# Step 0 of a gated scan loads f, k and q with four tokens a partition and works by halves of heads

## The chip, the cores and the metric

The kernel runs on one core of a Trainium2 chip. The metric is the device time in microseconds (us). A core has five engines that run side by side: TensorE (PE in the profile) multiplies matrices, VectorE (DVE), ScalarE (ACT) and GpSimd (POOL) work element by element, and SyncE (SP) issues transfers to the DMA queues. TensorE writes to eight PSUM banks of 128 x 512 floats. Everything else lies in SBUF, which has 128 partitions.

## The reference

A gated linear recurrence gives 384 features per token, and a gated two-layer network (ReGLU) follows. There are 4 batches, 8 heads, 768 tokens and head width 48; the network is 384 to 1536 to 384.

```python
f = 1.0 / (1.0 + np.exp(-f_logit))
state = np.zeros((B, H, D, D), dtype=np.float32)
for t in range(S):
    state = f[:, :, t, :, None] * state + np.einsum('bhd,bhe->bhde', k[:, :, t], v[:, :, t])
    y[:, :, t] = np.einsum('bhd,bhde->bhe', q[:, :, t], state)
# x: y with its heads side by side, (B*S, 384)
out = (np.maximum(x @ w_gate, 0.0) * (x @ w_val)) @ w_out
```

## The kernel before

The tokens are cut into six chunks of 128, here called steps 0 to 5, each for four batches. Within a chunk the recurrence is done as attention: the running sum L of -log f over the tokens comes from a product with a triangle of ones, q is scaled by exp(-L) and k by exp(L) (the "hats"), and the scores of q against k are masked by the triangle. y is the masked scores times v, plus q times the old state. The state is carried from step to step.

Nothing waits on an order found at run time. The program lists all operations with assumed durations, a small list scheduler (`Plan`) puts them in an order for each engine and gives them PSUM banks, and each engine then runs its list in that order, with semaphores where one needs another. So the assumed durations set the order, not the time.

For one batch of one step (`attention(c, b)`):

```python
sc.activation(fl, fl, AF.Exp, scale=-1.0)            # f: exp, then ln(1 + .)   [L416, L419]
sc.activation(bo, fl, AF.Ln, bias=1.0)
te.matmul(bc.ap[:, 0:HD], tri[:, :], bn[:, :, 0:D])  # running sums            [L426]
...                                                  # totals with "ones"      [L428]
sc.activation(ex[:, 1, :], bc.ap[:, 0:HD], AF.Exp, scale=1.0)    # for k       [L435]
sc.activation(ex[:, 0, :], bc.ap[:, 0:HD], AF.Exp, scale=-1.0)   # for q       [L437]
...                                                  # decay of the state      [L441]
hk = k * ex[:, 1];  hq = q * ex[:, 0]                # VectorE in step 0, else GpSimd [L447, L451]
gp.tensor_copy(vout, vin)                            # v, cast and padded      [L456]
if c < n_pe_transposed:      # 3                     # steps 0 to 2
    te.transpose(...)  # 8 of 128x128, k then q      [L466]
    ve.tensor_copy(qkT, tp)                          # out of PSUM             [L471]
else:                                                # steps 3 to 5
    sy.dma_start(qkT, hats, transpose=True)          # a DMA transposes        [L475]
te.matmul(s, kT, qT)   # 8, scores                   [L486]
ve.tensor_tensor(ptm, s, tri, ALU.mult)              # 2, mask                 [L492]
te.matmul(y, ...)      # from the old state and from v  [L514; L521 and L525 in steps 3 to 5]
sc.activation(xT, y, AF.Copy)                        # steps 0 to 2            [L532]
...                                                  # steps 3 to 5: copy [L539], then a DMA transposes [L541]
te.matmul(kv, hats_k, v)   # 4, new state            [L551]
...                                                  # step 0: VectorE [L561]; else VectorE, GpSimd [L565, L567]
```

The projections of a step take blocks j of 128 hidden features, 12 in all, with all four batches side by side (512 columns), in step 1 with two at a time (256):

```python
te.matmul(gate, wg_block, xT)  # 3    [L583]
sc.activation(relu, gate, AF.Relu)  # [L589]
te.matmul(val, wv_block, xT)   # 3    [L583]
ve.tensor_tensor(gT, relu, val, ALU.mult)  # [L593]
...
te.matmul(o, gT, wo)           # 12 a batch, output rows  [L604]
sc.activation(osb, o, AF.Copy)           # [L612]; stored by a DMA [L615]
```

The loads of step 0 are one DMA a batch and tensor (192 KB in rows of 48 floats), those of the later steps one for two batches (384 KB). The weights, nine parts of 384 KB in bf16, are issued by GpSimd (L370).

Of the kernel before, what the change touches and what calls it, by code (L numbers as in the profile page):

```python
# [11 lines left out]
class Op:  # L12
# [4 lines left out]
                 "after", "follows", "flow", "goal")  # L17

    def __init__(self, eng, emit, reads, writes, occ, lat, prio, opens=(), after=(), follows=()):
        self.eng, self.emit, self.reads, self.writes = eng, emit, reads, writes  # L20
        self.occ, self.lat, self.prio, self.opens = occ, lat, prio, list(opens)
        self.after, self.follows = list(after), list(follows)
        self.users = []
        self.inc = False
        self.sem = None
        self.val = 0
        self.start = None
        self.flow = None

# [11 lines left out]
class Plan:  # L41
# [4 lines left out]
    def __init__(self, limits):  # L46
        self.ops = []
        self.limits = limits

# [38 lines left out]
    def schedule(self, banks):  # L88
        self.link()
        for op in self.ops:  # L90
            op.n_left = len(op.deps)
            op.ready = 0.0
            for d in op.deps:
                d.users.append(op)
        free = {e: 0.0 for e in self.ENGINES}
# [5 lines left out]
        slots = [{"ap": ap, "tile": None, "at": 0.0} for ap in banks]  # L101
# [113 lines left out]
def bass_hgrn2_outer__then__ffn_reglu_kernel(  # L215
# [10 lines left out]
    n_pe_transposed = 3  # L226
    load_batches = 2
    flight = 3
    n_tiled = 3
    wsteps = 3  # L230
    early = ("f0.0.1 f0.1.2 f0.2.3 f0.3.4 k0.0.1 q0.0.1 v0.0.1 k0.1.2 q0.1.2 v0.1.2 k0.2.3 q0.2.3 "
             "v0.2.3 k0.3.4 q0.3.4 v0.3.4 wg0 wv0 wg1 wv1 wg2 wv2 f1.0.2 k1.0.2 q1.0.2 v1.0.2 wo0 wo1 "
             "wo2 f1.2.4 k1.2.4 q1.2.4 v1.2.4").split()
    lag = 3.0
    first_hats = ['DVE', 'DVE']
    groups = [(0,0,4,1),(1,0,2,0),(1,2,4,0),(2,0,4,0),(3,0,4,0),(4,0,4,0),(5,0,4,0)]
# [15 lines left out]
    NL = 3  # L252
    ld = {n: [sb(f"{n}_in{i}", [128, B, H, D], F32) for i in range(NL)] for n in "fkqv"}
    NB = 3
    bneg = [sb(f"bneg{i}", [128, 2, H, 64], BF16) for i in range(NB)]
    NE = 3
    expo = [sb(f"expo{i}", [128, 2, HD], F32) for i in range(NE)]
    NH = 6
    hats = [sb(f"hats{i}", [128, 2, H, 64], BF16) for i in range(NH)]
    NQ = 6  # L260
    qkT = [sb(f"qkT{i}", [128, 2, NP, C], BF16) for i in range(NQ)]
    NM = 3
    ptm = [sb(f"ptm{i}", [128, 2, NP, C], BF16) for i in range(NM)]
# [3 lines left out]
    NA = 8  # L267
    dec = [sb(f"dec{i}", [128, NP, 2], F32) for i in range(NA)]
    NN = 4
    xn = [sb(f"xn{i}", [128, HD], BF16) for i in range(NN)]  # L270
    NS = 4
# [12 lines left out]
    tri = sb("tri", [128, C], BF16)  # L284
    ident = sb("ident", [128, 128], BF16)
    ones = sb("ones", [128, 1], BF16)
    banks = [nc.alloc_psum_tensor(f"ps{i}", [128, 512], F32) for i in range(8)]

    pl = Plan({"bc": 1, "tp": 1, "s": 2, "y": 1, "kv": 1, "f": 4})
    add = pl.add  # L290
    gp, ve, sc, te, sy = nc.gpsimd, nc.vector, nc.scalar, nc.tensor, nc.sync

    def pe_t(*cols):
        return sum(max(n, 64) / 2400.0 + 0.0025 for n in cols)
# [3 lines left out]
    def act_t(n):  # L298
        return dict(occ=0.1 + n / 1200.0, lat=0.2)

    def dve_t(n):
        return dict(occ=0.08 + n / 960.0, lat=0.2)

    def pool_t(n):
        return dict(occ=0.15 + n * 2.2 / 1200.0, lat=0.2)


    add("POOL", lambda: gp.memset(tri[:], 1.0), [], ["tri"], occ=0.2, prio=-9)
    add("POOL", lambda: gp.affine_select(out=tri[:], in_=tri[:], compare_op=ALU.is_ge, fill=0.0, base=0,
                                         pattern=[[1, 128]], channel_multiplier=-1),  # L310
        ["tri"], ["tri"], occ=0.3, prio=-9)
    add("POOL", lambda: gp.memset(ident[:], 0.0), [], ["ident"], occ=0.2, prio=-8)
    add("POOL", lambda: gp.affine_select(out=ident[:], in_=ident[:], compare_op=ALU.not_equal, fill=1.0,
                                         base=0, pattern=[[-1, 128]], channel_multiplier=1),
        ["ident"], ["ident"], occ=0.3, prio=-8)
    add("POOL", lambda: gp.memset(ones[:], 1.0), [], ["ones"], occ=0.1, prio=-8)

    def zero(eng, e, t, name, cols, prio):
        add(eng, lambda: e.memzero(t), [], [name], occ=0.15 + cols / 2000.0, prio=prio)

    for i in range(NB):
        zero("DVE", ve, bneg[i][:], f"bneg{i}", 1024, -9)
    for i in range(NH):
        zero("DVE", ve, hats[i][:], f"hats{i}", 1024, -8)
    for i in range(NV):
        zero("POOL", gp, vpad[i][:], f"vpad{i}", VW, -7)
    for i in range(NA):
        zero("DVE", ve, dec[i][:], f"dec{i}", 2 * NP, -5)

# [4 lines left out]
    def dma(op, slot, flow):  # L334
# [3 lines left out]
        slots[slot][1] += 16  # L338
# [4 lines left out]

    def load(n, c, b0, b1, after=()):
        last = tails.get("load")
        t = ld[n][c % NL]
        src = bass.AP(tensor=srcs[n].tensor, offset=b0 * H * S * D + c * C * D,
                      ap=[[D, C], [S * D, (b1 - b0) * H], [1, D]])
        dst = t[:, b0:b1, :, :].rearrange("p b h d -> p (b h) d")
        op = add("SP", lambda: sy.dma_start(dst, src), [], [f"{n}{c % NL}_{b}" for b in range(b0, b1)],  # L350
# [3 lines left out]
        dma(op, f"{n}{c % NL}_{b0}{b1}", 1.03 * (b1 - b0))  # L354
# [5 lines left out]
    def load_w(nm, s, after):  # L360
# [4 lines left out]
        else:  # L365
# [4 lines left out]
        op = add("POOL", lambda: gp.dma_start(dst, src), [], [f"{nm}{s}"], occ=0.8, lat=1.0, prio=0, after=after,  # L370
                 follows=[last] if last else [])
        tails["load_w"] = op
        dma(op, f"{nm}{s}", 7.4 / wsteps)
        return op


    done = []
    for item in early:
        weight = item[0] == "w"
        cost, need = 0.0, []  # L380
        for other, flow, op in reversed(done):
            if cost >= lag and other != weight:
                need = [op]
                break
            cost += flow
        if weight:
            op = load_w(item[:2], int(item[2:]), need)
        else:
            c, b0, b1 = (int(x) for x in item[1:].split("."))
            op = load(item[0], c, b0, b1, need)  # L390
        done.append((weight, op.flow, op))
# [6 lines left out]


    def attention(c, b):  # L400
        w = c * B + b
        P = w * 10
        li = c % NL
        bi, bj = (w // 2) % NB, w % 2
        ei, hi, qi, mi, vi, ai = w % NE, w % NH, w % NQ, w % NM, w % NV, w % NA
        xi = c % NX
        fin, kin, qin, vin = (ld[n][li] for n in "fkqv")

        if c == 0:
            parts = [(b, b + 1)]  # L410
        else:
            parts = [(b, b + 2)] if b % 2 == 0 else []
        for b0, b1 in parts:
            fl = fin[:, b0:b1, :, :].rearrange("p b h d -> p (b h) d")
            keys = [f"f{li}_{x}" for x in range(b0, b1)]
            add("ACT", lambda: sc.activation(fl, fl, AF.Exp, scale=-1.0), keys, keys, prio=P,  # L416
                **act_t((b1 - b0) * HD))
            bo = bneg[bi][:, b0 % 2:b0 % 2 + b1 - b0, :, 0:D].rearrange("p b h d -> p (b h) d")
            add("ACT", lambda: sc.activation(bo, fl, AF.Ln, bias=1.0), keys + [f"bneg{bi}"],  # L419
                [f"bn{bi}_{x % 2}" for x in range(b0, b1)], prio=P, **act_t((b1 - b0) * HD))  # L420

        bn = bneg[bi][:, bj, :, :]
        bc = Bank("bc")

        def cum():
            te.matmul(bc.ap[:, 0:HD], tri[:, :], bn[:, :, 0:D])  # L426
            for p in range(NP):
                mm = te.matmul(bc.ap[:, HD + p:HD + p + 1],  # L428
                               bn[:, 2 * p:2 * p + 2, :].rearrange("p h d -> p (h d)"), ones[:, :])
            return mm  # L430
        chain("cum", "PE", cum, ["tri", "ones", f"bneg{bi}", f"bn{bi}_{bj}"], [bc], occ=0.48, lat=PE_L,
            prio=P, opens=[bc])

        ex = expo[ei]
# [3 lines left out]
            [f"expq{ei}"], prio=P + 1, **act_t(HD))  # L438
        if c < NC - 1:
            for j in range(2):  # L440
                add("ACT", lambda lo=64 * j, j=j: sc.activation(dec[ai][lo:lo + 64, :, j], bc.ap[lo:lo + 64, HD:HD + NP],  # L441
                                                                AF.Exp, scale=-1.0),
                    [bc, f"dec{ai}"], [f"dec{ai}_{j}"], prio=P + 2, **act_t(NP))

        hq, hk = hats[hi][:, 0, :, 0:D], hats[hi][:, 1, :, 0:D]
        e0 = first_hats[0] if c == 0 else "POOL"
        add(e0, lambda: (gp if e0 == "POOL" else ve).tensor_tensor(hk, kin[:, b, :, :], ex[:, 1, :].rearrange("p (h d) -> p h d", h=H),  # L447
                                             ALU.mult),
            [f"k{li}_{b}", f"expk{ei}", f"hats{hi}"], [f"hk{hi}"], prio=P + 2, **(pool_t(HD) if e0 == "POOL" else dve_t(HD)))
        e1 = first_hats[1] if c == 0 else "POOL"  # L450
        add(e1, lambda: (gp if e1 == "POOL" else ve).tensor_tensor(hq, qin[:, b, :, :], ex[:, 0, :].rearrange("p (h d) -> p h d", h=H),  # L451
                                             ALU.mult),
            [f"q{li}_{b}", f"expq{ei}", f"hats{hi}"], [f"hq{hi}"], prio=P + 2, **(pool_t(HD) if e1 == "POOL" else dve_t(HD)))
        vp = vpad[vi]
        vout = bass.AP(tensor=vp, offset=0, ap=[[VW, 128], [VSTEP, NP], [64, 2], [1, D]])
# [268 lines left out]
```

## Time and profile before

The median of three runs is 215.39 us (215.35 to 215.4); the profiled execution spans 212.0 us.

| engine | busy, us | share of the span | instructions |
|---|---|---|---|
| PE (matmul) | 186.4 | 88% | 1712 |
| PEld (weight loads, beside PE) | 107.2 | 51% | 1712 |
| DVE | 106.0 | 50% | 189 |
| ACT | 109.5 | 52% | 249 |
| POOL | 72.8 | 34% | 102 |

| queue | packets | MB | share of 16 engines |
|---|---|---|---|
| loads, stores, DMA transposes | 120320 | 27.93 | 64.4% |
| weights | 3984 | 3.54 | 11.2% |

A share of busy time is an average over stages. In the slice rows each digit is a fortieth of the span in tenths of busy time. In the chain each line is a start, a length and what ran or was waited for; "x8" is the number of instructions merged. Line numbers are those in brackets above.

### The profile page before, as it was taken

What the parts mean: (1) busy time and instruction counts of PE and PEld (TensorE: products, weight loads), DVE (VectorE), ACT (ScalarE), POOL (GpSimd) and SP (SyncE); (2) the same over time, 40 slices, a digit from 0 to 9 for tenths busy, and PEclk for the clock granted to TensorE, in tenths of its full rate; (3) what the DMA queues carried; (4) which work ended last, traced back from release to release, by engine and by line L of the source; (5) the groups of instructions that cost most, each with busy time, mean ns of one, the idle gap of its engine ahead of it and who ended that gap; (6) DMA issues with size and microseconds to landing.
All of it is one profiled execution on the core that took longest, in us unless ns stands there. A gap on an engine that the chain in (4) does not pass through costs nothing.

```text
span 212.0 us, 4302 instructions
## 1 busy us (share of the span) xinstructions
PE 186.4 (88%) x1712; PEld 107.2 (51%) x1712; DVE 106.0 (50%) x189; ACT 109.5 (52%) x249; POOL 72.8 (34%) x102
## 2 busy tenths in 40 slices
PE   0365699989999999997993899979999999999994
PEld 0254334455777766853551455535555544445562
DVE  7379525574196867464744357255633333333210
ACT  5940134836676958846753457555243344443411
POOL 3028102192658588853751636326000000000000
PEclk9999999999999999999999699999999999999999
DMA  6999999997999998999998998979422111111112
GB/s 120 217 206 165 196 207 227 152 201 157 200 245 184 188 226 181 172 229 178 212 187 166 216 174 187 184 162 209 111 56 59 37 37 37 40 37 37 37 44 104
DMA packets 124323, 31.73 MB, mean 150 GB/s; under 512 B 117392, under 2 KB 124304, under 8 KB 124304
## 3 DMA queue, kind: packets, MB, share of 16 engines
q1 hardware_dynamic: 120320, 27.93, 64.4%
q0 software_dynamic: 3984, 3.54, 11.2%
q8 instruction: 13, 0.21, 0.4%
q14 instruction: 6, 0.05, 0.1%
HBM read 25.95 MB, written 4.72 MB: 145 GB/s over the span
## 4 chain that ended last, share of the span: by engine, by line
PE 58%; DMA 13%; POOL 8%; ACT 8%; DVE 6%; issue 3%; SPq 2%; POOLq 0%
PE ps L583 30%; PE ps L604 18%; DMA qkT<-hats 7%; DMA f_in<-in_f_logit_dram 7%; POOL hats L451 3%; DVE ptm L492 3%; PE ps L466 3%; POOL hats L447 2%; PE ps L486 2%; ACT relu L589 2%; ACT expo L435 2%; PE ps L514 2%; DVE qkT L471 2%; ACT f_in L416 1%; SPq L350 1%
## 5 line engine op out<-in xcount | busy, mean ns | idle before, releaser
L593 DVE TENSOR_TENSOR gT<-relu,ps 128x512 bf16<-128x512 bf16 (+1 forms) x84 | 50.8, 610 | 63.0 <-PE ps L583 52.9
L589 ACT ACTIVATE relu<-ps 128x512 bf16<-128x512 f32 (+1 forms) x84 | 44.8, 536 | 35.8 <-PE ps L583 35.6
L583 PE MATMUL ps<-xT,wg 128*128 128x512 bf16 (+1 forms) x252 | 61.8, 355 | 0.6 <-ACT xT L532 0.6
L583 PE MATMUL ps<-xT,wv 128*128 128x512 bf16 (+1 forms) x252 | 61.8, 354 | 0.0
L604 PE MATMUL ps<-wo,gT 128*128 128x384 bf16 x288 | 51.4, 326 | 0.0
L492 DVE TENSOR_TENSOR ptm<-ps,tri 128x512 bf16<-128x512 f32 x48 | 30.8, 684 | 14.1 <-PE ps L486 13.9
L604 PEld LDWEIGHTS ps<-wo,gT 128*128 128x128 bf16 x288 | 27.3, 98 | 18.1
L583 PEld LDWEIGHTS ps<-xT,wg 128*128 128x128 bf16 x252 | 23.5, 99 | 21.2 <-issue 1.7
L583 PEld LDWEIGHTS ps<-xT,wv 128*128 128x128 bf16 x252 | 23.3, 98 | 19.2 <-issue 1.3
L612 ACT ACTIVATE osb<-ps 128x384 f32<-128x384 f32 x24 | 11.8, 490 | 31.6 <-PE ps L604 31.5
L447 POOL TENSOR_TENSOR hats<-k_in,expo 128x384 bf16<-128x384 f32 x20 | 20.0, 999 | 20.1 <-ACT expo L435 20.1
L451 POOL TENSOR_TENSOR hats<-q_in,expo 128x384 bf16<-128x384 f32 x20 | 19.9, 998 | 8.6 <-DMA q_in<-in_q_dram 8.6
L567 POOL TENSOR_TENSOR st<-ssum,dec 128x384 bf16<-128x384 f32 x16 | 13.2, 830 | 18.9 <-DVE ssum L565 18.7
L486 PE MATMUL ps<-qkT 48*128 48x128 bf16 x192 | 10.4, 233 | 8.0 <-DMA qkT<-hats 6.7
L435 ACT ACTIVATE expo<-ps 128x384 f32<-128x384 f32 x24 | 11.8, 491 | 8.8 <-PE ps L428 8.7
L426 PE MATMUL ps<-bneg,tri 128*128 128x384 bf16 x24 | 8.6, 359 | 8.4 <-ACT bneg L419 8.4
L456 POOL CAST vpad<-v_in 128x384 bf16<-128x384 f32 x24 | 12.3, 531 | 10.5 <-DMA v_in<-in_v_dram 10.5
L532 ACT ACTIVATE xT<-ps 128x384 bf16<-128x384 f32 x12 | 5.9, 492 | 16.6 <-PE ps L514 16.2
L471 DVE COPY qkT<-ps 128x1024 bf16<-128x1024 bf16 x12 | 8.3, 689 | 12.0 <-PE ps L466 11.9
L486 PEld LDWEIGHTS ps<-qkT 48*128 48x128 bf16 x192 | 5.9, 100 | 14.3 <-DMA qkT<-hats 8.6
L416 ACT ACTIVATE f_in<-f_in 128x768 f32<-128x768 f32 (+1 forms) x14 | 10.4, 747 | 4.5 <-DMA f_in<-in_f_logit_dram 4.2
L437 ACT ACTIVATE expo<-ps 128x384 f32<-128x384 f32 x24 | 11.8, 494 | 0.0
(39 smaller groups left out, 126.3 us busy)
## 6 DMA issues: line engine op xcount, KB each, us to landing
out_dram<-osb SPq DMA_DIRECT2D x24, 192.0 KB, 2.1
f_in<-in_f_logit_dram SPq DMA_DIRECT2D x10, 384.0 KB, 5.5
k_in<-in_k_dram SPq DMA_DIRECT2D x10, 384.0 KB, 5.3
q_in<-in_q_dram SPq DMA_DIRECT2D x10, 384.0 KB, 4.7
v_in<-in_v_dram SPq DMA_DIRECT2D x10, 384.0 KB, 5.1
wg<-in_moe_w_gate_dram POOLq DMA_DIRECT2D x3, 384.0 KB, 7.2
wv<-in_moe_w_val_dram POOLq DMA_DIRECT2D x3, 384.0 KB, 8.3
wo<-in_moe_w_out_dram POOLq DMA_DIRECT2D x3, 384.0 KB, 6.2
```

What stands on the lines that cost most here:

```text
L416: add("ACT", lambda: sc.activation(fl, fl, AF.Exp, scale=-1.0), keys, keys, prio=P, **act_t((b1 - b0) * HD))
L435: add("ACT", lambda: sc.activation(ex[:, 1, :], bc.ap[:, 0:HD], AF.Exp, scale=1.0), [bc], [f"expk{ei}"], prio=P + 1, **act_t(HD))
L447: add(e0, lambda: (gp if e0 == "POOL" else ve).tensor_tensor(hk, kin[:, b, :, :], ex[:, 1, :].rearrange("p (h d) -> p h d", h=H), ALU.mult ...
L451: add(e1, lambda: (gp if e1 == "POOL" else ve).tensor_tensor(hq, qin[:, b, :, :], ex[:, 0, :].rearrange("p (h d) -> p h d", h=H), ALU.mult ...
L471: add("DVE", lambda: ve.tensor_copy(qkT[qi][:, :, :, :].rearrange("p x n t -> p (x n t)"), tp.ap[:, :].bitcast(BF16)), [tp], [f"qkT{qi}"], ...
L486: mm = te.matmul(s.ap[:, p * C:(p + 1) * C], qkT[qi][lo:lo + D, 1, p, :], qkT[qi][lo:lo + D, 0, p, :])
L492: add("DVE", lambda j=j, s=s: ve.tensor_tensor(ptm[mi][:, j, :, :], s.ap[:, :].rearrange("p (n t) -> p n t", n=NP), mask, ALU.mult), [s, " ...
L567: add("POOL", lambda: gp.tensor_tensor(t4(s_new), t4(tmp), rate, ALU.mult), [key] + dk, [f"S{b}_{c % 2}"], prio=P + 8, **pool_t(HD))
L583: mm = te.matmul(bank.ap[:, 0:n], wt[:, kt, j * 128:(j + 1) * 128], xT[xi][:, kt, n0:n1], start=(kt == 0), stop=(kt == NK - 1))
L589: add("ACT", lambda: sc.activation(relu[ri][:, 0:n], gate.ap[:, 0:n], AF.Relu), [gate], [f"relu{ri}"], prio=P, **act_t(n))
L593: add("DVE", lambda: ve.tensor_tensor(gT[gi][:, j, n0:n1], relu[ri][:, 0:n], val.ap[:, 0:n], ALU.mult), [val, f"relu{ri}"], [f"gT{gi}_{j}_ ...
L604: mm = te.matmul(o.ap[:, 0:DM], gT[gi][:, j, b * C:(b + 1) * C], wo[:, j, :], start=(j == 0), stop=(j == NJ - 1))
```

## The change

Its aim is to have the first inputs of the projections sooner and TensorE's clock up when they come, and to plan with other durations.

1. In step 0 f, k and q come with four consecutive tokens of one head in one row of 768 bytes; partition 4r + b holds tokens 4r to 4r + 3 of batch b. All four batches are then worked together, in two halves of four heads. v stays as it was.
2. The running sums of step 0 need two masks for that (`upto`, `below`): ones only where row and column belong to the same batch. k's part of the hats is turned back to natural order later (`attention_back`), when y is done, for the state.
3. TensorE multiplies zeros in the gaps of its plan up to 17 us.
4. The projections of step 0 do blocks 0 to 3 for two batches at a time, the others for four; step 1 blocks 0 to 5 for two, the others for four. The output rows of step 0 are made for two batches together, weight part by weight part.
5. Weights and inputs of step 1 are issued in another order, at other planned times; buffers are counted anew (f two steps, k, q, v two and a half, before three), banks are allotted anew, and the assumed durations are changed.

```diff
-    early = ("f0.0.1 f0.1.2 f0.2.3 f0.3.4 k0.0.1 q0.0.1 v0.0.1 ... wg0 wv0 wg1 wv1 wg2 wv2 f1.0.2 ...").split()
+    first = ("f0 k0 q0 v0.0 v0.1 wg0~8.0 wv0~8.5 wg1~14.5 wv1~15.3 wg2~17.5 wv2~18.3 f1.0@wv1 k1.0 q1.0 v1.0 "
+             "wo0~23 wo1~25.5 f1.1@wo0 k1.1 wo2~28 q1.1 v1.1").split()
...
-    NL = 3
+    NL = {"f": 4, "k": 5, "q": 5, "v": 5}
...
-    pl = Plan({"bc": 1, "tp": 1, "s": 2, "y": 1, "kv": 1, "f": 4})
+    pl = Plan({"bc": 2, "bc4": 4, "tp": 2, "tp4": 4, "s": 4, "y": 2, "kv": 1, "f": 4})
...
-        return dict(occ=0.1 + n / 1200.0, lat=0.2)
+        return dict(occ=0.17 + n / 1150.0, lat=0.2)
...
+    def load_four(n, c):
+            for b in range(B):
+                src = bass.AP(tensor=srcs[n].tensor, offset=b * H * S * D + c * C * D,
+                              ap=[[4 * D, 32], [S * D, H], [1, 4 * D]])
+                dst = bass.AP(tensor=t, offset=b * row + slot_of(n, c, 0) * 2 * HD, ap=[[4 * row, 32], [4 * D, H], [1, 4 * D]])
+                ops.append(sy.dma_start(dst, src))
...
+    def attention_four(c):
+        for hh in range(2):                # halves of heads
+            ... Exp, Ln of 128 x 768
+        for hh in range(2):
+            for z in range(2):             # pairs of the four tokens
+                ... 5 products: upto or below, by bn[:, o]
+            for z in range(2):
+                ... Exp for q to SBUF, Exp for k in its bank
+                e = "DVE" if z else "POOL"
+                ... hats of q by e, hats of k by DVE
+            for x in (1, 0):
+                ... 8 transposes; copy of k's by DVE, of q's by ACT
+            for b in range(0, B, 2):
+                ... 8 scores of two batches, two masks by DVE
+        for j in range(2):
+            masks[(0, 2, j)].follows.append(masks[(1, 0, 1)])
...
+    def attention_back(c, b, behind):
+        ... 4 transposes of k, one copy by DVE, planned behind the batches' y
...
-            dma(op, f"qkT{qi}", 0.9)
+            dma(op, f"qkT{qi}", 1.5)
...
-            dma(op, f"xT{xi}_{b}", 0.35)
+            dma(op, f"xT{xi}_{b}", 0.55)
...
-    groups = [(0,0,4,1),(1,0,2,0),(1,2,4,0),(2,0,4,0),(3,0,4,0),(4,0,4,0),(5,0,4,0)]
+    groups = {0: [(0, 2, range(0, WJ)), (2, 4, range(0, WJ)), (0, 4, range(WJ, NJ))],
+              1: [(0, 2, range(0, 6)), (2, 4, range(0, 6)), (0, 4, range(6, NJ))]}
...
+    warm_until = 17.0
+    def warm():
+        return te.matmul(spare[:, 0:WARM], zeros[:, 0:128], zeros[:, 0:WARM], start=True, stop=True, skip_group_check=True)
+    for op in order["PE"]:
+        gap, each = op.start - at, 0.44 if at < 4.5 else 0.23
+        if begun and op.start <= warm_until:
+            for _ in range(int((gap - 0.05) / each)):
+                busy.append((op, warm))
```

(The lines with "..." behind the plus sign stand for code that is described and cut. Step 5 leaves out the totals that only a next step needs.)

## The prediction

> **What bounds the kernel now.** I read the busy digits by slice first, then the chain of waits in order of time, then the sums by stretch, then the DMA queues. The slices of the page:
>
> ```profile
> PE   0365699989999999997993899979999999999994
> DVE  7379525574196867464744357255633333333210
> PEclk9999999999999999999999699999999999999999
> DMA  6999999997999998999998998979422111111112
> ```
>
> One slice is 5.3 us. TensorE is hardly used in the first five slices and full in nearly all others, so the time is (when the projections start) + (TensorE's work from there) + (its holes) + a tail. The DMA row is full to about 150 us: data arrives only just fast enough, and a shift of TensorE to earlier times must be checked against it. When the projections start is in the chain:
>
> ```profile
> 1.32 3.60 DMA f_in<-in_f_logit_dram
> ...
> 14.53 0.98 PE ps L466 x8
> 15.53 0.69 DVE qkT L471
> ...
> 24.25 1.30 DVE ptm L492 x2
> 25.59 0.65 PE ps L514 x15
> 26.27 0.50 ACT xT L532
> 26.82 13.74 PE ps L583 x57
> ...
> 155.90 1.95 PE ps L604 x12
> 157.85 3.88 PE ps L583 x18
> ```
>
> The first projection is at 26.82, when the fourth batch of step 0 has gone through its transposes, copy, scores, mask and y one after the other. The unhindered rates are in the last two lines: 3.88/18 = 0.2156 us for a 512-column product and 1.95/12 = 0.1625 for a 384-column one. By stretches, TensorE alone (stretch, length, busy and instructions, granted clock, DMA share, GB/s):
>
> ```profile
> 26.80:40.00 13.20, 13.19 (x56) 1.00 1.18 204
> 40.00:60.00 20.00, 19.23 (x226) 1.00 0.93 187
> 60.00:80.00 20.00, 19.74 (x342) 1.00 1.07 209
> 80.00:100.00 20.00, 18.50 (x208) 1.00 1.05 185
> 100.00:120.00 20.00, 15.97 (x149) 0.95 0.97 195
> 120.00:140.00 20.00, 19.87 (x156) 0.96 0.90 177
> 140.00:160.00 20.00, 18.68 (x164) 1.00 0.65 136
> 160.00:180.00 20.00, 20.00 (x105) 1.00 0.11 40
> ```
>
> Empty between 26.8 and 160: 0.0+0.8+0.3+1.5+4.0+0.1+1.3 = 8.0 us, half of it at 100 to 120, where the list of waits has scores waiting for the DMA that transposes q and k.
>
> Check of the budget: projections 360 x 0.2156 + 144 x 0.108 (256 columns; 0.325 for three in the timeline) + 288 x 0.1625 = 140 us. Attention of steps 1 to 5 on TensorE from the chain's pieces (sums 0.25, transposes 0.45, scores 0.33, y 0.50 or 0.37, state 0.17 a batch): 8 x 1.70 + 12 x 1.12 = 27 us. 26.8 + 140 + 27 + 8 holes + tail 2.9 (last product ends at 209.1) = 204.7; the span is 212.0. The missing 7 us are slow clock (below) and small gaps between pieces. The measured time is 3.4 over the span; I add this at the end.
>
> **What the Trainium skill says.** "TensorE: Matmul & The Clock Gate", Part 1 (the HAM clock gate): the array starts at half clock and is released by some 3.4 us of steady activity, and idling throttles it again. The trace agrees: eight transposes take 0.98 us on the chain at 14.53 but 0.45 at 56.93, and the first nine projections take about 0.42 us each until 29.3 instead of 0.216. The granted-clock row doesn't show this start; the durations do. "DMA: Bandwidth & Descriptors", Specifications, gives 512 B as the smallest transfer for line rate. The trace agrees in kind: 117392 of 124323 packets are under 512 B, and full DMA gives 185 to 209 GB/s, while in 160 to 180, with little but 1536-byte output rows, 40 GB/s keep it 0.11 busy, 364 GB/s per busy time. "SBUF — State Buffer", Who interferes with whom, says that VectorE and GpSimd share one port pair as an exclusive lock. In step 0 of before hardly anything on GpSimd meets VectorE, so no number here; the change puts two products of step 0 on GpSimd.
>
> **The change, part by part.**
>
> *Loads of f, k, q in step 0.* Before: 12 loads of 192 KB in 192-byte rows, 1024 packets each. The queue has 120320 packets for 64.4% of 16 x 212 us, 18.2 ns each, so 12 x 1024 x 18.2/16 = 14.0 us of all engines. After: 3072 packets of 768 B. I estimate 300 GB/s, under the 364 above as the rows are half as long: 2.36 MB/300 = 7.9 us. Saved: 5 to 6 us of DMA. But f now arrives whole: first issue at 0.8, about 2 us until data lands, 2.6 of transfer: 5.2 instead of 3.7. k by 7.9, q by 10.6, v (unchanged form) by 15.
>
> *Step 0 by halves of heads.* ScalarE: exp and ln of two halves, 4 x 0.84 = 3.4 (before 8 x 0.52 = 4.1). From 5.2: the first half's sums start at 6.9, ln of the second is done at 8.6, then eight exps of 0.49 and two q copies of about 1.0. VectorE: four k products and two q products 0.56, two copies 0.69, eight masks 0.68 = 10.2 us, as against 8 x 0.56 + 4 x 0.69 + 8 x 0.68 + 4 x 0.55 = 14.9 before; state updates are put behind. By hand: k products of half 0 at 9.6 and 10.7, transposes 11.4 to 12.6, copies to 13.7, scores to 14.2, masks of batches 0 and 1 to 15.6; half 1 follows about 2 us behind on VectorE, so its masks for batches 0, 1 end near 16.8 to 17.4. y (0.3 each), copies of y 0.5 each: the first two batches are ready at **about 18.5**, batches 2 and 3 at about 21 (four more masks, 2.7). The first four hidden blocks of batches 0, 1 take 4 x 6 x 0.108 = 2.6 us, just bridging that. First projection: 26.8 - 18.5 = **8.3 us earlier**.
>
> *Zeros on TensorE.* They stand in planned gaps up to 17 us and warm the clock. The cold start of the projections costs 2.53 us at half rate, 1.3 us, and goes. (Step 0's own pieces get faster too: in the 18.5.) A filler is 0.22 us, so one too many delays little.
>
> *Put behind.* For four batches k goes back through TensorE: 16 transposes, 2 x 0.45 = 0.9, and the state products, 4 x 0.17 = 0.7, which lay before 26.8. They now lie in the full part: **+1.6**. Step 5 saves its ones-products, 4 x 0.08 = 0.3.
>
> *Splits and row pairs.* Step 1 is cut into halves for six blocks only; 2 x 0.108 = 0.216, so nothing either way. The output products of step 0 by pairs of batches are the same products, only waiting longer for each weight part: 0.
>
> *The order.* The kernel is a fixed order made from assumed durations. The q/k DMA transpose goes from 0.9 to 1.5 of assumed transfer, y's from 0.35 to 0.55; the page has 3.8 and 2.6 us to landing. TensorE should then meet late scores less often. Holes and rewarming cost 8 + 2 us (products at 118 to 121 run at half rate); I expect 2 us back.
>
> Sum: -8.3 - 1.3 + 1.6 - 0.3 - 2 = -10.3, if supply keeps up.
>
> *Supply.* In before the inputs of step 1 are issued up to 50.9 and land about 5 us later, 56. Saving 5 to 6 us brings this to about 50, while TensorE comes 8 to 9 us earlier: projections of step 0 need 15.6 us of hidden work from 18.5, to 34, and then the output weights, which must squeeze past step 1's inputs. By bytes, 3.1 MB of step 0, six weight parts and half of step 1 come ahead; landing is near 38. A hole of 2 to 4 us near 34 to 45 is likely, partly filled by the put-behind work. I charge **+1.5**, net of what the later phases hide again. 215.4 - 10.3 + 1.5 = 206.6; I round down to **206.3**, since the new constants fit the trace (0.17 + 384/1150 = 0.50 us for an exp that takes 0.49; before it assumed 0.42).
>
> **Rivals.** (1) *DMA becomes the bound and keeps the gain.* For it: the full DMA row to 150, 18.9 MB of inputs in 192-byte rows of which only an eighth changes. Against: after 160 TensorE has 50 us of work and idle DMA, and the transposes of step 5's y wait in the queue for projections at 154. Time then: only the 5 us of DMA, 210. (2) *The new order is worse:* inputs have buffers for 2 or 2.5 steps instead of 3, scores and sums may hold more banks against the projections, and waits fixed in the wrong order cost 2 to 4 us each, as at 117. Time: 208 to 213. (3) *Step 0 isn't faster:* f, k and q are awaited whole, products in steps of four tokens may read or write slower, and ScalarE gains two copies. First projection at 22, time 210. (4) *The order is much better:* most of the 8 us of holes go: 200 to 202.
>
> **Range and chances.** The start is uncertain by 2 us, holes by 4 us either way, supply by 2. Together: **201 to 210.8**. Over 2% faster is under 211.1: to miss it, half of the gain must be lost in new holes. Faster 0.89, within 2% 0.08, slower 0.03.
>
> **What would show it.** First projection at 17.5 to 20 and at 0.11 us per 256 columns from the start; f landing near 5, q by 11; 768-byte packets at about 300 GB/s. Then few holes at 100 to 120, and one or two at 34 to 58 ended by output weights or step-1 inputs. I am wrong if the first projection is after 21, if TensorE's holes after it exceed 11 us, or if they are under 4.

## The result and the profile after

The changed kernel takes 209.64 us (median; 208.53 to 210.33) against 215.39 us (215.35 to 215.55) before: a ratio of 0.974 with a 95% interval of 0.969 to 0.979. The profiled execution spans 208.5 us, 3.5 less than before. Its first projection, however, comes at 29.28 us, 2.5 us *later* than before.

The slices of the changed kernel's page:

```profile
PE   7835779999999799999999999997999999999994
...
PEclk9995758999999999999999999999999999999999
DMA  4997899999599999999889999988961111111112
```

TensorE is busy in the first two slices now, mostly with zeros, and then empty for most of the third (3). The DMA row has a dent in the fourth and fifth slices (7 and 8), where TensorE's clock is low too (5 and 7). Why the start is late is in the chain of waits, in order of time:

```profile
8.17 7.36 DMA q_in<-in_q_dram
...
18.00 1.89 PE ps L555 x16
19.89 2.56 PE ps L880 x6
22.45 1.04 PE ps L574 x15
...
29.28 2.10 PE ps L796 x9
```

The chain waits 7.36 us for q of step 0, from its last issue at 8.17 us to 15.53. The first transposes come at 18.00. Six products of zeros (L880) at half rate, 0.43 us each, stand in front of the scores (L574), and the first nine projections (L796, 256 columns) take 2.10 us where the full rate gives 9 x 0.108 = 0.97.

What makes up for it lies behind. TensorE by stretches (stretch, length, busy and instructions, granted clock, DMA share, GB/s):

```profile
26.80:40.00 13.20, 11.71 (x150) 0.76 1.26 198
...
60.00:80.00 20.00, 18.84 (x313) 1.00 1.02 205
80.00:100.00 20.00, 19.73 (x227) 1.00 1.13 197
100.00:120.00 20.00, 19.84 (x189) 1.00 0.95 176
120.00:140.00 20.00, 19.74 (x140) 1.00 0.99 193
140.00:160.00 20.00, 18.34 (x148) 1.00 0.70 138
```

From 60 to 160 us TensorE is empty for 1.2 + 0.3 + 0.2 + 0.3 + 1.7 = 3.5 us, as against 7.2 in the same stretches of before. The granted clock stays at 1.00 from 100 to 140, where before had 0.95 and 0.96. A simple figure separates the two halves: the span less the time of the first projection. It is 212.0 - 26.8 = 185.2 us before and 208.5 - 29.3 = 179.2 after. The part behind the first projection got 6.0 us shorter, the part ahead of it 2.5 longer. Both figures come from one execution each. The spans differ by 3.5 us and the median times by 5.75: the changed kernel's profiled execution is its longest (210.33), and the span of before lies 3.4 us under its median time, where every other execution on record lies 1.7 to 1.9 under its own. So the profiled execution of before was some 1.6 us faster than its median (an estimate), the 3.4 us that the prediction adds at the end is no fixed amount, and differences of 1 to 2 us between such figures say little.

### The profile page after: what moved, and what is told of

It reads as the page before. It is cut to its first block, busy times and chain, and to the rows that moved or that the text cites. A ratio compares the mean times of both kernels' runs of the same rounds, so it can differ in the third digit from the quotient of the medians.

```text
span 208.5 us, 4328 instructions
## 1 busy us (share of the span) xinstructions
PE 191.4 (92%) x1724; PEld 110.0 (53%) x1743; DVE 105.1 (50%) x183; ACT 110.5 (53%) x239; POOL 79.6 (38%) x112
## 2 busy tenths in 40 slices
DMA packets 115076, 31.74 MB, mean 152 GB/s; under 512 B 105072, under 2 KB 115056, under 8 KB 115056
## 4 chain that ended last, share of the span: by engine, by line
PE 84%; DMA 5%; SPq 3%; DVE 2%; ACT 2%; issue 2%; DVEq 0%
PE ps L796 45%; PE ps L819 22%; DMA q_in<-in_q_dram 4%; SPq L385 3%; PE ps L706 3%; PE ps L733 2%; PE ps L767 2%; PE ps L676 2%; PE ps L640 2%; DMA qkT<-hats 1%; PE ps L555 1%; PE ps L880 1%; PE ps L743 1%; PE ps L739 1%; PE ps L574 1%
## 5 line engine op out<-in xcount | busy, mean ns | idle before, releaser
L796 PE MATMUL ps<-xT,wv 128*128 128x512 bf16 (+1 forms) x243 | 60.1, 355 | 0.3 <-issue 0.2
L796 PE MATMUL ps<-xT,wg 128*128 128x512 bf16 (+1 forms) x231 | 57.5, 355 | 1.4 <-ACT xT L750 0.6
L819 PE MATMUL ps<-wo,gT 128*128 128x384 bf16 x288 | 52.1, 326 | 0.0
L796 PEld LDWEIGHTS ps<-xT,wg 128*128 128x128 bf16 x246 | 23.1, 99 | 20.0 <-ACT xT L750 0.9
L796 PEld LDWEIGHTS ps<-xT,wv 128*128 128x128 bf16 x246 | 22.9, 98 | 19.9
L711 DVE TENSOR_TENSOR ptm<-ps,tri 128x512 bf16<-128x512 f32 x40 | 26.0, 685 | 9.3 <-PE ps L706 9.3
L650 ACT ACTIVATE expo<-ps 128x384 f32<-128x384 f32 x20 | 9.8, 491 | 2.4 <-PE ps L643 2.2
L480 DVE TENSOR_TENSOR ssum<-ps,st 128x384 f32<-128x384 f32 x16 | 8.9, 553 | 4.3 <-PE ps L767 4.2
L652 ACT ACTIVATE expo<-ps 128x384 f32<-128x384 f32 x20 | 9.9, 495 | 0.0
L631 ACT ACTIVATE f_in<-f_in 128x768 f32<-128x768 f32 x10 | 8.4, 840 | 2.6 <-DMA f_in<-in_f_logit_dram 2.6
L706 PE MATMUL ps<-qkT 48*128 48x128 bf16 x160 | 7.9, 219 | 1.8 <-DMA qkT<-hats 1.5
L880 PE MATMUL ps<-zeros 128*128 128x512 bf16 x24 | 9.3, 538 | 0.1
L756 ACT ACTIVATE xn<-ps 128x384 bf16<-128x384 f32 x12 | 5.9, 488 | 5.2 <-PE ps L743 5.2
```

What stands on the lines that cost most here:

```text
L706: mm = te.matmul(s.ap[:, p * C:(p + 1) * C], tokens(c, b, 1, p, lo, lo + D), tokens(c, b, 0, p, lo, lo + D))
L711: add("DVE", lambda j=j, s=s: ve.tensor_tensor(ptm[mi][:, j, :, :], s.ap[:, :].rearrange("p (n t) -> p n t", n=NP), mask, ALU.mult), [s, " ...
L796: mm = te.matmul(bank.ap[:, 0:n], wt[:, kt, j * 128:(j + 1) * 128], xT[xi][:, kt, n0:n1], start=(kt == 0), stop=(kt == NK - 1))
L819: mm = te.matmul(o[b].ap[:, 0:DM], gT[gi][:, j, b * C:(b + 1) * C], wo[:, j, :], start=(j == 0), stop=(j == NJ - 1))
L880: return te.matmul(spare[:, 0:WARM], zeros[:, 0:128], zeros[:, 0:WARM], start=True, stop=True, skip_group_check=True)
```

## The experiments

Each was measured against the kernel before on the same chip, whose median was 214.8 us beside e1 to e4, 215.2 beside e5 to e8 and 213.4 beside e9 to e11. The intervals of the ratios allow for that.

| kernel | us | ratio to before (95%) | first projection | from there to the end |
|---|---|---|---|---|
| before | 215.39 | 1 | 26.8 | 185.2 |
| changed | 209.64 | 0.974 (0.969 to 0.979) | 29.3 | 179.2 |
| e1 changed, weights behind q | 207.89 | 0.967 (0.961 to 0.972) | 25.5 | 180.8 |
| e2 changed, no zeros | 209.07 | 0.972 (0.966 to 0.978) | 29.1 | 177.3 |
| e3 before, new durations | 208.03 | 0.970 (0.965 to 0.976) | 26.4 | 179.7 |
| e4 changed, old transpose times | 216.87 | 1.010 (1.005 to 1.016) | 29.3 | 185.4 |
| e5 before, new transpose times only | 209.23 | 0.968 (0.957 to 0.980) | | |
| e6 before, other new times only | 210.72 | 0.984 (0.975 to 0.994) | 25.7 | 183.1 |
| e7 changed, first step replanned | 203.71 | 0.952 (0.945 to 0.959) | 22.4 | 180.4 |
| e8 e7 with zeros to 21 us | 202.88 | 0.948 (0.939 to 0.957) | 22.1 | 179.7 |
| e9 e8, weights not held | 205.04 | 0.963 (0.959 to 0.967) | 27.0 | 176.3 |
| e10 e8, no zeros | 203.89 | 0.956 (0.951 to 0.961) | 23.2 | 179.5 |
| e11 e8 again | 201.98 | 0.950 (0.943 to 0.957) | 21.7 | 178.4 |

The last two columns are of the profiled executions. Runs more than 1.5% above the fastest of their kernel (one of four in e2, two of four in e5, some of before) are in the medians but not in the ratios, and e5's profiled execution is one of them, so its last two columns are empty.

### Where the gain came from: e3 and e4

e3 is the kernel *before* with other assumed durations in its planner and nothing else:

```diff
-        return dict(occ=0.1 + n / 1200.0, lat=0.2)      # ScalarE
+        return dict(occ=0.17 + n / 1150.0, lat=0.2)
-        return dict(occ=0.08 + n / 960.0, lat=0.2)      # VectorE
+        return dict(occ=0.14 + n / 950.0, lat=0.2)
 ...                                                     # GpSimd, sums, transposes, y, state likewise
-            dma(op, f"qkT{qi}", 0.9)
+            dma(op, f"qkT{qi}", 1.5)
-            dma(op, f"xT{xi}_{b}", 0.35)
+            dma(op, f"xT{xi}_{b}", 0.55)
```

> The kernel before with nothing changed but the assumed durations of the planner (elementwise, sums, transposes, y, state, and 1.5 and 0.55 for the DMA transposes). Theory A (the gain of the change comes from the new durations, which order TensorE's work with fewer holes after 60 us, 3.5 instead of 7.2): holes from 60 to 160 fall to 3 to 5 us and the time to 209.5 to 212. Rival B (the holes go because of the new first step, the banks and the buffers): holes 6 to 9 us, time 213.5 to 217.

It takes 208.03 us, less than theory A allowed. The whole gain is there without the new first step. Banks, buffers, splits and the order of the loads were not varied one by one; all that the changed kernel has beyond e3, the first step among it, makes no difference that can be told (0.970 and 0.974, the intervals overlap). Its stretches from 100 us on:

```profile
100.00:120.00 20.00, 17.16 (x161) 0.92 0.97 191
120.00:140.00 20.00, 19.83 (x157) 1.00 0.89 180
140.00:160.00 20.00, 19.75 (x163) 1.00 0.63 143
```

Empty are 2.8 + 0.2 + 0.3 us, and 60 to 100 adds 0.2: 3.5 us, as many as in the changed kernel.

e4 is the counterpart: the changed kernel with the two former transfer times.

```diff
-            dma(op, f"qkT{qi}", 1.5)      # and 1.3 -> 1.2 to issue
+            dma(op, f"qkT{qi}", 0.9)
-            dma(op, f"xT{xi}_{b}", 0.55)
+            dma(op, f"xT{xi}_{b}", 0.35)
```

> The changed kernel with the former assumed transfer of the DMA transposes, 0.9 and 0.35 instead of 1.5 and 0.55; all else as changed, so only the order from step 3 on differs. Theory A (this number removed the waits of scores for transposed q and k between 98 and 142 us): these waits come back, 3 to 5 us more of holes, time 212 to 215. Rival B (other parts did): holes within 1 us of the changed kernel's 3.5 and time 208.5 to 210.5.

It takes 216.87 us, more than theory A allowed and over the kernel before. The same stretches, and the longest hole in TensorE's timeline (start, length, what ran; in brackets the idle time before it and what ended it):

```profile
100.00:120.00 20.00, 17.64 (x168) 1.00 0.93 182
120.00:140.00 20.00, 16.47 (x120) 1.00 0.90 181
140.00:160.00 20.00, 19.22 (x156) 0.91 0.64 139
```

```profile
140.31 0.40 PE L706 MATMUL ps<-qkT 48*128 48x128 bf16 x8 [3.05 <-DMA qkT<-hats]
```

6.7 us are empty here, as against 2.1 in the changed kernel. Scores (L706) of steps 3 to 5 wait for a DMA's transpose of q and k, the kind of hole that before has at 100, 113, 117 and 141. These waits in all (us, times, longest), first in e4, then in the changed kernel:

```profile
PE ps L706 <- DMA qkT<-hats: 5.4, 4, 3.1
PE ps L706 <- DMA qkT<-hats: 1.5, 2, 1.3
```

They account for 3.9 of the 6.2 us that the part behind the first projection loses. That part takes 185.2 us with the old step and all old times, 179.7 with the old step and all new times (e3), 179.2 with the new step and all new times. e4 has the new step with old transpose times but all other times new; its counterpart with the old step is e6 below: 185.4 against 183.1. So the transposes' times are worth 6.2 us beside the new step and 3.4 beside the old one, and with all times new the two steps differ by 0.5 us. The times decide, the first step doesn't.

### Which of the durations: e5 and e6

e5 takes only the transposes' part of e3's diff, e6 only the rest.

> The kernel before with two assumed numbers changed: transfer of the DMA transposes 1.5 and 0.55 instead of 0.9 and 0.35 (and 1.3 instead of 1.2 to issue). Theory A (these two numbers are the gain, as putting them back in the changed kernel cost 7 us): time 207.5 to 210, and from the first projection to the end 179 to 181 us instead of 185. Rival B (it takes the elementwise durations too): 211 to 215.

> The kernel before with all the new assumed durations but those of the two DMA transposes. Theory A (the transposes' numbers alone are the gain): 213 to 217, waits of scores for transposed q and k from 98 to 142 us as in before. Rival B (the other durations carry part of it): 209 to 212.

By the ratios e5 gains 3.2% and e6 1.6%, e3 with both 3.0%. Theory A held for e5's time (its figure for the part behind the first projection is not shown) and fell for e6: the other durations alone also help, to 210.72. TensorE's waits for transposed q and k, in before, e6 and e3:

```profile
PE ps L486 <- DMA qkT<-hats: 6.7, 4, 2.4
PE ps L486 <- DMA qkT<-hats: 4.1, 3, 2.0
PE ps L486 <- DMA qkT<-hats: 0.9, 2, 0.6
```

The two parts don't add: the other durations alone already shorten these waits. That the transposes' two numbers are the larger part isn't shown, as the intervals of e5 and e6 overlap.

### Why the start is late: e1 and e2

The changed kernel's timeline at the place (L419 issues weights, L538 makes the q product):

```profile
7.92 0.94 POOL L419 DMA_DIRECT2D wg<-in_moe_w_gate_dram  x1
...
8.86 0.78 POOL L419 DMA_DIRECT2D wv<-in_moe_w_val_dram  x1
...
15.61 2.26 POOL L538 TENSOR_TENSOR hats<-q_in,expo 128x384 bf16<-128x384 f32 x2 [5.97 <-DMA q_in<-in_q_dram]
15.62 1.40 DVE L538 TENSOR_TENSOR hats<-q_in,expo 128x384 bf16<-128x384 f32 x1 [10.64 <-DMA q_in<-in_q_dram]
```

GpSimd issues two weight parts at 7.9 and 8.9 us, while q's four transfers are being issued (6.2 to 8.8). VectorE's first product of the step is one of q, and the products of k stand behind it in the order: it waits 10.6 us for q, by the list of waits. e1 keeps every order and adds one wait:

```diff
+            if op is done["wg0"]:
+                eng.wait_ge(done["q0"].sem, done["q0"].goal)
```

> The changed kernel in the same order on every engine; only the first weight transfer (and with it all later ones) waits until q of step 0 has landed. Theory A (the two weight transfers issued at 7.9 and 8.9 us share the DMA engines with q and hold it back from about 12 to 15.5 us): q lands at 11.5 to 12.5, the first projection comes 2.5 to 4 us earlier than its 29.3, and the time falls to 205 to 207.5. Rival B (q is late of itself, as three tensors in 768-byte rows take that long): q still lands after 14.5, the first projection stays at 28.5 to 30, and the time is 209 to 212.

```profile
8.18 4.70 DMA q_in<-in_q_dram
...
12.96 0.56 DVE L538 TENSOR_TENSOR hats<-q_in,expo 128x384 bf16<-128x384 f32 x1 [7.99 <-DMA q_in<-in_q_dram]
13.18 0.94 POOL L419 DMA_DIRECT2D wg<-in_moe_w_gate_dram  x1 [5.22 <-DMA q_in<-in_q_dram]
...
25.46 0.82 PE L796 MATMUL ps<-xT,wg 128*128 128x256 bf16 x3 [0.76 <-ACT xT L750]
```

q lands at 12.9 instead of 15.5 us: from its last issue 4.7 us instead of 7.36. So the weights under way beside it held it back. The first projection comes 3.8 us earlier. Of that, 1.75 us arrive in the median time. q and the time miss the ranges of theory A by 0.4 us each, and the intervals of e1 and the changed kernel overlap a little, so the earlier start is shown and the gain in time is likely only.

e2 takes the zeros out:

```diff
-        if begun and op.start <= warm_until:
+        if False and begun and op.start <= warm_until:
```

> The changed kernel without the products of zeros between other work (the first one stays), same order. Theory A (in the order as it runs the zeros do no good: the clock is throttled from 17 to 23 us all the same, and six zeros at half rate, 2.6 us, stand before the scores): first projection 1 to 1.5 us earlier, time 1 us lower, 208 to 209.2. Rival B (they keep the clock up where it matters, as intended): time 0.5 to 2 us higher, 210 to 211.5.

209.07 us: no difference that can be measured, and the first projection is earlier by 0.2 us, not by 1 to 1.5. Without zeros the clock is at half from 18 to 26.8 (0.50 against 0.69), so what the six zeros cost ahead of the scores the slower pieces cost instead. The time lies in theory A's range, but the start that was to bring it doesn't come, and rival B's loss isn't there either: as planned, the zeros neither help nor harm measurably.

### A first step planned as the trace shows it: e7 to e11

e7 changes three things in the changed kernel, which together let the k products run while q is under way:

```diff
-        dma(op, f"{n}{slot_of(n, c, 0)}", 2.4, 4)
+        dma(op, f"{n}{slot_of(n, c, 0)}", {"f": 2.4, "k": 3.2, "q": 3.2}[n], 4)
-            op = load_w(item[:2], int(item[2:]), float(at))
+            op = load_w(item[:2], int(item[2:]), float(at), [done["q0"]] if item == "wg0" else [])
-                e = "DVE" if z else "POOL"
+                e = "DVE"
```

> The changed kernel with its first step planned as the trace shows it: the weights wait for q, k and q are assumed to land as late as they do, so VectorE makes the k products while q is under way, and all q products are on VectorE, none on GpSimd. Theory A (the start of the projections sets the end): first projection 23 to 24.5 instead of 29.3 (25.5 with the waiting weights alone), time 205 to 207. Rival B (from here the supply of weights and of step 1 sets the end, not the start): first projection as early, but new holes between 26 and 60 us and time 207.5 to 209.

203.71 us and a first projection at 22.4, both under the ranges of theory A. e8 also has `warm_until = 21.0`:

> As e7, with zeros planned up to 21 instead of 17 us. Theory A (zeros help if they reach up to the first projection): no half-rate projections at the start and time 0.5 to 1.3 us under e7. Rival B (zeros in a fixed order delay what comes after them as much as they speed it): within 0.5 us of e7 or above it.

Its timeline (k products, q products, the first projection) and its stretches:

```profile
11.29 1.02 DVE L543 TENSOR_TENSOR hats<-k_in,ps 128x384 bf16<-128x384 f32 x2 [6.32 <-ACT ps L535]
...
12.43 1.03 DVE L538 TENSOR_TENSOR hats<-q_in,expo 128x384 bf16<-128x384 f32 x2
...
22.12 0.50 PE L796 MATMUL ps<-xT,wg 128*128 128x256 bf16 x3 [0.76 <-ACT xT L750]
```

```profile
26.80:40.00 13.20, 13.20 (x91) 1.00 1.13 188
40.00:60.00 20.00, 20.00 (x276) 1.00 0.97 209
```

k's products are at 11.3, q's at 12.4, and the projections begin at 22.1, the first six products at full rate; from 24 to 26 us the granted clock is at 0.50 all the same. From 26.8 to 60 us TensorE has no hole at all: the projections being 7 us earlier don't outrun the weights or step 1's inputs. Rival B of e7 is out.

e8 takes 202.88 us, 0.8 less than e7, as theory A wanted; but the intervals overlap and the half rate isn't gone, so what the longer zeros are worth beside e7 isn't shown. Once more, beside e9 and e10, it takes 201.98 us with a first projection at 21.7, both a little under what was expected. By the median it is the fastest of all kernels here.

> e8 once more, on the same chip as the two others, so that they can be compared: 202 to 204 us, first projection at 22 to 22.5.

e9 is e8 with the weights free (the `load_w` line of the diff as in the changed kernel):

> As e8 (replanned first step, all q products on VectorE, zeros to 21 us), but the weights don't wait for q: GpSimd issues them from 8 us on, and as it has no q products now, four of them at once. Theory A (the weights' share of the DMA engines is the first cause of the late start): q lands at 15.5 us or later, the first projection comes 3 to 5 us after that of e8 (22.1), time 205 to 208. Rival B (the order on VectorE was the cause, the waiting weights only a part): first projection at 22 to 23.5, time 202 to 204.5, as the weights also land earlier.

```profile
15.86 1.03 DVE L538 TENSOR_TENSOR hats<-q_in,expo 128x384 bf16<-128x384 f32 x2 [4.41 <-DMA q_in<-in_q_dram]
...
25.62 0.77 PE L733 MATMUL ps<-ptm,vpad 128*32 128x128 bf16 x32 [1.28 <-POOL vpad L697]
27.02 0.50 PE L796 MATMUL ps<-xT,wg 128*128 128x256 bf16 x3 [0.62 <-ACT xT L750]
```

The k products are done early, at 10.4, but q lands at 15.9 and the first projection is at 27.0, 5.3 us after e11's on the same chip; the time is 3.1 us longer, and the intervals (0.959 to 0.967 against 0.943 to 0.957) don't meet. Theory A held. In e9 v is late too (y, L733, waits for v's cast at 25.0), as four weight parts are under way there and only two in the changed kernel. From the changed kernel to e11 the start moves by 29.3 - 21.7 = 7.6 us. Holding the weights back is worth 3.8 of them when it is done first (e1) and 5.3 when it is done last (e9 to e11), so half or more of the late start is the weights. The rest, the order on VectorE, q's products off GpSimd and more zeros, is worth 2.3 to 3.8 us; these three weren't tried one by one.

e10 is e8 without zeros (the diff of e2):

> As e8, without any zeros between other work. Theory A (with an order that fits, zeros are worth having): the pieces of step 0 run at half rate, first projection 1 to 2 us later than 22.1 and at half rate, time 1 to 2.5 us over e8. Rival B (they are worth nothing measurable, as in e2): within 0.7 us of e8.

The first projection is at 23.2, 1.5 us after e11's, and the time is 1.9 us longer; the intervals overlap, so the loss of start is shown and the loss of time is likely only. Nor do the zeros do all they are for. e11's stretches:

```profile
20.00:22.00 2.00, 0.89 (x34) 0.85 1.23 201
22.00:24.00 2.00, 2.00 (x21) 0.50 1.24 206
```

Between 20 and 22 us TensorE waits for masks and then for the copies of y, is busy 0.89 us of 2, and the clock falls to 0.50 just when the projections begin.

## Why the prediction was right, and where it was wrong

The time fell within the range, and faster by over 2% was right. But the sum came out for the wrong reason, by luck: the start is 10.8 us later than predicted, and the part behind it is much shorter than predicted. Two of the prediction's own signs of being wrong came true: the first projection is after 21, and the holes after it are 3.8 us, under 4.

- **"First projection: 8.3 us earlier" failed.** It is 2.5 us later. The step that failed is "k by 7.9, q by 10.6". Two things were missing from it. First, the issue: each of the twelve transfers takes the queue's issuer 0.61 to 0.75 us, so q's last one is issued at 8.17. Even with the weights held back (e11's chain, below) it lands 3.86 us later, at 12.0; f lands near 6.2 instead of 5.2. I had counted bytes only. Second, the weights under way beside it: another 2.6 us in e1, 3.8 between e11 and e9. I counted the weights in the supply of the projections, not in the time before q. And "k products of half 0 at 9.6 and 10.7" took the data's order, where the planned order put a q product first; the diff has q's priority *after* k's, but the planner takes what it believes to be ready first. With both put right, e11's first projection is still 3.2 us after 18.5; q gives 1.4 of them, and eleven zeros stand on its chain for 2.5, though without them (e10) it comes later still.

```profile
8.18 3.86 DMA q_in<-in_q_dram
...
21.74 2.10 PE ps L796 x9
```

- **"Zeros ... 1.3 us, and goes" failed.** The first nine projections ran at half rate all the same; e2 shows no effect on the time. (The prediction counts nine such products in before; 2.53 us at 0.42 are six, and the 1.3 us are right.)
- **"+1.6 put behind" was about right.** The transposes back (L613) take 1.2 + 0.2 us, partly at half rate, and the state products (L767) 4 x 0.17: 2.1.
- **"I expect 2 us back" from the order had the right mechanism and a wrong size.** The stretch from the first projection to the end shrank by 6.0 us although 2.1 us were moved into it and its start stayed cold; putting back the transposes' numbers costs 6.2 us of it and 7.2 us of time (e4). The kernel before gains 3.0% from the new times alone (e3). I had this as rival 4, "most of the 8 us of holes go", but coupled it to an early start.
- **"Supply +1.5" failed.** In e8, with a start at 22.1, there is no hole from 26.8 to 60; for a start at 18.5 it stays open. But part of an earlier start is given back: e9, which begins 5.3 us after e11, needs 2.1 us less from there on, and its time is 3.1 us longer.
- **Rival 1** (DMA keeps the gain, 210) names the measured time but not its cause: e8 moves the same 31.74 MB and is 7 us faster, so DMA was not yet the bound. **Rival 3** ("f, k and q are awaited whole ... first projection at 22, time 210") was the nearest to what happened to the start, and too mild; 22 is about what e7, e8 and e11 reach with the weights held and the order put right.

Had the start come as predicted, 18.5 + 179.2 would have made a span of 197.7 us (an estimate, as an earlier start is partly given back); e11, which begins at 21.7, has 200.1.

## What to carry to other kernels

In a kernel whose order is fixed ahead of time, the assumed durations are part of the program: two numbers for DMA transposes moved the time by 3.2% in the kernel before (e5) and in the changed one by 3.6% of before's time (e4), while the rewritten first step as planned moved nothing that can be told. That truer durations always help isn't shown: e4, with truer times for all but the transposes, is slower than before, and no other values were tried. Compare the plan with the trace first at the places where an in-order engine waits while it has other work, and change the order there. And look at what else is on the DMA engines while the transfer is under way on which the first stage waits: one wait that kept the weights back until q had landed brought the first projection 3.8 us (e1) and 5.3 us (e9 to e11) forward.

## What the runs showed of the hardware beyond what I expected

- Rows of 768 bytes ran at 254 to 264 GB/s in the two-microsecond stretches from 4 to 8 us (changed kernel and e1), rows of 192 bytes at 188 to 230 there in before; I had estimated 300. The DMA engines were 0.89 to 0.95 busy with the long rows, so per busy time these ran at 278 to 294 GB/s, the short ones at about 200. The time to issue fell much less than the packets: 0.61 us for a transfer of 256 packets, 0.71 to 1.2 for one of 1024. The packets alone don't set it: the load of f issued at 28.47 in the changed kernel, 384 KB in 192-byte rows, took 0.37.
- A product on VectorE (L538, both operands in SBUF) took 1.40 us while GpSimd ran the same operation, and 0.56 us alone (e1). Products of k (L543), which read one operand from PSUM, took 0.54 us also while GpSimd still ran. The Trainium skill, "SBUF — State Buffer", Who interferes with whom, says that they exclude each other on a shared port pair; the longer time agrees with that.
- The granted-clock row read 1.00 at the start of before, where products ran at half rate until 29.3 us, but showed 0.50 in the changed kernel from 18 to 22. So a row at full is no proof of full rate before the first dense stretch; durations are.
